# A linear-attention and MLP kernel: batch elements in the row halves of TensorE, attention products on 64x64 quarters, and another draw of the planned order

## The chip, the cores and the metric

The kernel runs on one core of a Trainium2 chip. The core has a matrix engine (TensorE, called PE in the profile), a vector engine (VectorE, DVE), a scalar engine (ScalarE, ACT), a general-purpose engine (GpSimd, POOL) and an engine for synchronisation and DMA issue (SyncE, SP). Each works through its own queue of instructions in order; semaphores tie the queues together. The metric is the time of one execution on the device in microseconds (us).

## The reference

For each of 4 batch elements and 8 heads, a 64x64 state is carried over 768 time steps with a decay per head, and read out with the query:

```python
gamma = 1.0 - 2.0 ** (-5.0 - np.arange(H))
for t in range(S):
    state = gamma * state + einsum('bhd,bhe->bhde', k[:, :, t], v[:, :, t])
    y[:, :, t] = scale * einsum('bhd,bhde->bhe', q[:, :, t], state)
x = y.transpose(0, 2, 1, 3).reshape(B * S, H * D)      # 3072 x 512
h = x @ w_in                                           # 3072 x 2048
out = (h * cos(h)) @ w_out                             # 3072 x 512
```

Inputs and the output are float32; the kernel multiplies in bf16.

## The kernel before

**Tiling.** The recurrence is taken in chunks of 128 time steps, 6 per batch element. A *pair* is one chunk of two batch elements, so there are 12 pairs (`NP`). The decay is folded into q and v (`conv_q`, `conv_v`, by the tables `gq` and `gk`), so that inside a chunk the output is the masked product (Q K^T) V, and what comes from earlier chunks is Q times the state. For each pair the kernel

- loads q, k and v, and converts them to bf16 (`conv_q` L282 and `conv_v` L286 mostly on POOL, `conv_k` on ACT);
- transposes q and k to put the head dimension on the partitions (`qkt`): pairs 0 to 5 on PE (`t_mm`, L308) with a copy out of PSUM (`t_copy`), later pairs by DMA transposes in SP's queue (`dma_t`, L297);
- forms A = K Q^T for the eight heads of both elements (`a_mm`, L331), with two heads in the two row halves of PE, each 64 rows by 128 columns;
- masks A into bf16 (`a_mask`, L337, DVE);
- forms Y = state Q + V A (`y_mm`, L362 and L367) in column halves, 128 rows by 64 columns; the state stands in 128x128 blocks with zeros off the diagonal, `stb`;
- adds to the state in PSUM (`s_mm`, L387, 128x64) and copies it out (`s_copy`);
- copies Y out to `xt` (`y_copy`, ACT).

Two pairs make a *group* of 512 tokens, which runs through the MLP: `f_mm` (L401; `h_mm`, L422, for half a group early on), the cosine on ACT (`f_cos`, L409), the product on DVE (`f_mul`, L413), and the output projection `o_mm` (L446), whose result goes out through `o_out`.

**What sets the order.** Pairs 0 to 5, the transposes and A of pair 6 and the first MLP group are put in order by a planner written in the kernel (`Plan`): each operation has an engine, a cost, a rank and its inputs, the planner simulates the engines, and the operations are emitted by planned start. While PE waits early on, the planner inserts matmuls on zeros (`idle_mm`, L472). The rest is a loop written out by hand: 16 steps per group, each with four matmuls of F for one group and four of O for the group before it, and in every eighth step `block(p)`: A of pair p+1, then Y of pair p, its copies, S, the state copy and the masks. `conv(p + 2)` and the loads of pair p+4 follow. The waits among engines come from the data that instructions share.

**Buffers.** PSUM has seven banks in rotation (`Banks`) and one for the state. q, k, v and `qkt` in bf16 have three sets each, the loads five, the outputs four (`ob`). In the planned part all loads are issued from POOL's queue, between its conversions.

Of the kernel before, what the change touches and what calls it, by code (L numbers as in the profile page):

```python
# [28 lines left out]
class Plan:  # L29
# [33 lines left out]
    def run(self, start, cold_until=0.0, look=0.0, fill=None):  # L63
# [5 lines left out]
        t = 0.0  # L69
        while left:  # L70
            nxt = []
            for e in "SPADE":
# [4 lines left out]
                soon = 1e9  # L77
                for op in left:
# [5 lines left out]
                    if r > t + 1e-9:  # L84
                        nxt.append(r)
                        if op["rank"] < 20:
                            soon = min(soon, r)
                        continue
# [14 lines left out]
                if e == "E" and best and best[0][0] >= 1000 and soon < t + look:  # L103
                    best = None
                if best is None:
# [35 lines left out]

    def emit(self):
        for op in sorted(self.ops, key=lambda o: (o["start"], o["n"])):
            op["fn"](op["eng"])


HALF0, SPARE, RF, RM, COLD = 4, 1, 40.0, 40.0, 5.2
# [3 lines left out]
def kernel(  # L151
# [39 lines left out]
    st_ps = psum.tile([128, 2, HP, D], FP32, name="st_ps")  # L191
# [13 lines left out]
    qs = [sb([128, 2, H, D], BF16, f"qs{i}") for i in range(NB)]  # L205
    ks = [sb([128, 2, H, D], BF16, f"ks{i}") for i in range(NB)]
    vs = [sb([128, 2, H, D], BF16, f"vs{i}") for i in range(NB)]
    qkt = [sb([128, 2, 2, HP, 128], BF16, f"qkt{i}") for i in range(NB)]
    am = [[[sb([128, HP, 128], BF16, f"am{i}_{b}_{j}") for j in range(2)]
           for b in range(2)] for i in range(2)]  # L210
    stb = [sb([128, 2, HP, 128], BF16, f"stb{i}") for i in range(2)]
# [3 lines left out]
    kx = sb([128, 2, H, D], BF16, "kx")  # L215
# [10 lines left out]
    dec = gtf[:, 2048:4096].bitcast(FP32).rearrange("p (j a t) -> p j a t", j=2, a=HP)  # L226
# [4 lines left out]

    def kb(p):
        return kx if p == 1 else ks[p % NB]
# [6 lines left out]
    def load(eng, p, names):  # L240

        bp, c = divmod(ORDER[p], NC)
        for n in names.split():
            t, src = SRC[n[0].lower()]
            if len(n) == 1:
                t = (qs[p % NB] if n == "Q" else kb(p)) if n in "QK" else t[p % PRE]
# [31 lines left out]
    def conv_q(p, b, e):  # L278
        if p < 2:
            copy(e, qs[p % NB][:, b], qf[p % PRE][:, b])  # L280
            return
        ENG[e].tensor_tensor(out=qs[p % NB][:, b], in0=qf[p % PRE][:, b],  # L282
                             in1=bc(gq, ORDER[p] % NC), op=ALU.mult)
# [8 lines left out]
    def conv_k(p, b, e):  # L292
        copy(e, ks[p % NB][:, b], kf[p % PRE][:, b])

    def dma_t(p, w):
        n = p % NB
        nc.sync.dma_start_transpose(  # L297
            out=qkt[n][:, w].rearrange("p b a t -> p (b a) t"),
            in_=(qs, ks)[w][n].rearrange("p b h d -> p (b h d)"))
# [3 lines left out]
    def t_mm(p, b, w):  # L303
        if w == 0:
            held["t", p, b] = banks.take()
        tr = held["t", p, b].bitcast(BF16).rearrange("p (w a t) -> p w a t", w=2, a=HP)
        for a in range(HP):
            nc.tensor.transpose(  # L308
                tr[:, w, a, :], (kb(p) if w else qs[p % NB])[:, b, 2 * a : 2 * a + 2, :], ident)

    def t_copy(p, b, w, e):
        bank = held["t", p, b]
        tr = bank.bitcast(BF16).rearrange("p (w a t) -> p w a t", w=2, a=HP)
        copy(e, qkt[p % NB][:, w, b], tr[:, w])
        if w == 1:
            banks.give(bank)

    def qt(n, b, a):
        return qkt[n][:, 0, b, a, :]

    def kt(n, b, a):
        return qkt[n][:, 1, b, a, :]

    def a_mm(p, b):
        n = p % NB
        bk = held["a", p, b] = [banks.take(), banks.take()]
        ap = [t.rearrange("p (a t) -> p a t", a=HP) for t in bk]
        for a in range(HP):
            for j in range(2):
                po = 64 * j  # L330
                nc.tensor.matmul(ap[j][:, a, :], lhsT=kt(n, b, a)[po : po + 64, :],  # L331
                                 rhs=qt(n, b, a)[po : po + 64, :],
                                 tile_position=(po, 0))

    def a_mask(p, b, j):
        bank = held["a", p, b][j]
        nc.vector.tensor_tensor(  # L337
            out=am[p % 2][b][j], in0=bank.rearrange("p (a t) -> p a t", a=HP),
            in1=(dec[:, j] if p < 2 else mask.unsqueeze(1).to_broadcast([128, HP, 128])),
# [3 lines left out]
    def a_save(p, b, j):  # L343
        bank = held["a", p, b][j]
        nc.scalar.copy(out=amf[b], in_=bank)
        banks.give(bank)

    def a_late(p, b, j):
        nc.gpsimd.tensor_tensor(out=am[p % 2][b][j],
                                in0=amf[b].rearrange("p (a t) -> p a t", a=HP),  # L350
                                in1=dec[:, j], op=ALU.mult)

    def y_mm(p, b):
        c = ORDER[p] % NC
        n = p % NB
        bank = held["y", p, b] = banks.take()
        v_ = vr[p] if p < 2 else vs[n]
        yp = bank.rearrange("p (a t) -> p a t", a=HP)
        for a in range(HP):
            if c > 0:  # L360
                for j in range(2):
                    nc.tensor.matmul(  # L362
                        yp[ts(j, 64), a, :], lhsT=stb[p % 2][:, b, a, ts(j, 64)],
                        rhs=qt(n, b, a), start=True, stop=False,
                        skip_group_check=True)
            for j in range(2):
                nc.tensor.matmul(  # L367
                    yp[ts(j, 64), a, :], lhsT=v_[:, b, 2 * a + j, :],
                    rhs=am[p % 2][b][j][:, a, :], start=(c == 0), stop=True,
                    skip_group_check=True)  # L370
# [10 lines left out]
    def s_mm(p):  # L381
        x = 1 if p == LATE else p
        for b in range(2):
            for a in range(HP):
                for j in range(2):
                    h = 2 * a + j
                    nc.tensor.matmul(  # L387
                        st_ps[ts(j, 64), b, a, :], lhsT=kb(x)[:, b, h, :],
                        rhs=vb(x)[:, b, h, :],
                        start=(ORDER[x] % NC == 0 and b == 0 and a == 0),  # L390
                        stop=True, skip_group_check=True)

    def s_copy(p, j, e):
        copy(e, stb[(max(p, 1) + 1) % 2][ts(j, 64), :, :, ts(j, 64)], st_ps[ts(j, 64)])
# [54 lines left out]
    def o_out(g, j, e):  # L449
# [5 lines left out]
        nc.sync.dma_start(out=out[ds(o_row(g, j), C), :], in_=o)  # L455
# [46 lines left out]
    for j in range(2):  # L502
        for a in range(HP):
            nc.scalar.activation(out=dec[:, j, a, :], in_=dist, func=AF.Exp, bias=lnsc,
                                 scale=float(lg[2 * a + j]))
# [9 lines left out]
    CQ, CD = "D", "P"  # L515
    SPLIT = {(1, 0, 1), (0, 1, 1)}
    HOLD = "q2", "o2"
# [40 lines left out]
    for i in range(2):  # L558
        T["z", i] = add("D", 0.53, lambda e, i=i: nc.vector.memset(stb[i], 0.0), (), 1500, name="z%d" % i)
    for p in range(PL + 2):  # L560
# [26 lines left out]
        if p < DMA_T:  # L587
            for b in range(2):
                for w, x in enumerate("qk"):
                    T["t" + x, p, b] = add(  # L590
                        "E", 0.225, lambda e, p=p, b=b, w=w: t_mm(p, b, w),
                        [T["c" + x, p, b]] + ([T["tq", p, b]] if w else []), 10 * p + 1,
                        [("bank", 1)] if w == 0 else [], (), "full", name="t%s%d%d" % (x, p, b))
                for w, x in enumerate("qk"):
                    T["e" + x, p, b] = add(
                        "DA", SB2, lambda e, p=p, b=b, w=w: t_copy(p, b, w, e),
                        [T["t" + x, p, b], T.get(("eq", p, b)) if w else None] + old,
                        10 * p + 0.5, (), [("bank", 1)] if w else [], name="e%s%d%d" % (x, p, b))
            kq = {b: [T["eq", p, b], T["ek", p, b]] for b in range(2)}
        else:  # L600
# [4 lines left out]
            kq = {b: [T["dt", p, 0], T["dt", p, 1]] for b in range(2)}  # L605
        if p > PL:
            continue
        ms = []
        if p < ASEP:
            for b in range(2):  # L610
                T["a", p, b] = add("E", 0.225, lambda e, p=p, b=b: a_mm(p, b), kq[b], 10 * p + 2,
                                   [("bank", 2)], (), "row", name="a%d%d" % (p, b))
        else:
            T["a", p, 0] = T["a", p, 1] = add(
                "E", 0.445, lambda e, p=p: (a_mm(p, 0), a_mm(p, 1)), kq[0] + kq[1], 10 * p + 2,
                [("bank", 4)], (), "row", name="a%d" % p)
        for b in range(2):
            for j in range(2):
                if (p, b, j) in SPLIT:
                    o = add("A", (0.49, 0.585), lambda e, p=p, b=b, j=j: a_save(p, b, j),  # L620
                            [T["a", p, b]], 0, (), [("bank", 1)],
                            name="ms%d%d%d" % (p, b, j))
                    T["m", p, b, j] = add("P", (1.1, 1.2), lambda e, p=p, b=b, j=j: a_late(p, b, j),
                                          [o], 0, [("port", 1)], [("port", 1)],
                                          name="ml%d%d%d" % (p, b, j))
                    continue
                T["m", p, b, j] = add("D", (0.6, 0.69), lambda e, p=p, b=b, j=j: a_mask(p, b, j),
                                      [T["a", p, b], G("y", p - 2, b)], 10 * p + 1 + b,
# [158 lines left out]
```

## Time and profile before

| | |
|---|---|
| median of 3 runs | 212.67 us (212.4 to 212.92) |
| the profiled execution's own time | 212.12 us |
| its span, first to last instruction | 210.3 us |
| PE busy | 205.1 us (98%), 1726 matmuls |
| DVE, ACT, POOL busy | 116.2, 115.7, 80.0 us |
| O, L446 | 368 matmuls, 128x512 |
| F, L401 / L422 | 304 of 128x512 / 160 of 128x256 |
| A, L331 | 192 matmuls of 64x128 tiles |
| Y, L362 + L367 | 160 + 192 matmuls of 128x64 tiles |
| S, L387 | 160 matmuls of 128x64 tiles |
| matmuls on zeros, L472 | 62 |

In the page's rows of digits each digit is the busy share, in tenths, of one of 40 slices of the span (5.26 us each). In a timeline the first number is the start in us from the span's start, the second the time to the last end; then engine, line, operation, tiles written and read, the shape and the count. Matmuls are pipelined, and their ends are modelled, so the lengths of neighbours overlap and the distance from start to start is what one costs. For SP the rows are DMA issues by its queue ("SPq").

### The profile page before, as it was taken

The numbers are of one execution on the slowest core, as the hardware profiler recorded it, in microseconds if no ns is written. First come the engines' busy times: TensorE is split into PE (matmuls) and PEld (weight loads), VectorE is DVE, ScalarE is ACT, GpSimd is POOL, SyncE is SP. The second block draws the span as 40 slices with busy tenths as digits, with TensorE's granted clock in tenths as the row PEclk, the third lists the DMA queues.
The fourth block names the chain that finished last, engine by engine and source line by source line (L and its number), as shares of the span: only waits on it lengthen the run. The fifth ranks groups of instructions, "written<-read, shape, count | busy, mean of one in ns | idle before, by whom it ended". The sixth has DMA issues, their size and how long they took to land.

```text
span 210.3 us, 4279 instructions
## 1 busy us (share of the span) xinstructions
PE 205.1 (98%) x1726; PEld 112.9 (54%) x1726; DVE 116.2 (55%) x199; ACT 115.7 (55%) x193; POOL 80.0 (38%) x84
## 2 busy tenths in 40 slices
PE   7999999999999999999999999999999999999993
PEld 3777457888565445445445445445444444444462
DVE  7465899988664547647647647647642333333000
ACT  7767869878472347547546546545545554553120
POOL 8969999979999034635033000000000000000000
PEclk9999999999999999999999999999999999999998
DMA  7999999999999399999973303301101101110212
GB/s 118 195 255 230 304 321 218 212 338 345 345 254 204 105 229 255 258 220 246 216 200 103 92 8 104 95 4 55 48 2 53 50 0 50 50 55 10 90 72 78
DMA packets 57492, 32.00 MB, mean 152 GB/s; under 512 B 46592, under 2 KB 51968, under 8 KB 57472
## 3 DMA queue, kind: packets, MB, share of 16 engines
q0 software_dynamic: 14352, 15.47, 33.4%
q1 hardware_dynamic: 42976, 16.13, 30.5%
q8 instruction: 13, 0.21, 0.4%
q10 hardware_dynamic: 144, 0.13, 0.2%
q14 instruction: 7, 0.06, 0.1%
HBM read 27.26 MB, written 6.29 MB: 160 GB/s over the span
## 4 chain that ended last, share of the span: by engine, by line
PE 80%; DMA 7%; POOL 7%; ACT 2%; issue 1%; DVE 1%; POOLq 0%; DVEq 0%; ACTq 0%
PE bank L446 38%; PE bank L401 27%; DMA vf<-in_v_dram 7%; PE bank L422 5%; PE bank L362 2%; PE bank L331 2%; PE bank L367 2%; PE bank L463 2%; PE bank L308 1%; POOL qf L247 1%; POOL kf L247 1%; POOL vs L286 1%; ACT cosb L409 1%; PE st_ps L387 1%; POOL w_in_sb L258 1%
## 5 line engine op out<-in xcount | busy, mean ns | idle before, releaser
L409 ACT ACTIVATE cosb<-bank,halfpi 128x512 bf16<-128x512 f32 x96 | 65.5, 688 | 58.6 <-PE bank L401 54.0
L446 PE MATMUL bank<-w_out_sb,gt 128*128 128x512 bf16 x368 | 90.9, 379 | 0.0
L413 DVE TENSOR_TENSOR gt<-bank,cosb 128x512 bf16<-128x512 f32 x76 | 51.6, 689 | 54.0 <-ACT cosb L409 53.7
L401 PE MATMUL bank<-xt,w_in_sb 128*128 128x512 bf16 x304 | 77.1, 379 | 0.0
L446 PEld LDWEIGHTS <-gt 128*128 128x128 bf16 x368 | 35.6, 98 | 42.3
L401 PEld LDWEIGHTS <-w_in_sb 128*128 128x128 bf16 x304 | 28.8, 98 | 33.6
L286 POOL TENSOR_TENSOR vs<-vf,gk 128x512 bf16<-128x512 f32 x22 | 22.7, 1048 | 11.1 <-PE st_ps L387 4.8
L337 DVE TENSOR_TENSOR am<-bank,mask 128x512 bf16<-128x512 f32 x40 | 25.0, 683 | 1.8 <-PE bank L331 1.6
L282 POOL TENSOR_TENSOR qs<-qf,gq 128x512 bf16<-128x512 f32 x18 | 18.5, 1044 | 18.7 <-DMA qf<-in_q_dram 18.6
L271 ACT COPY ob<-bank 128x512 f32<-128x512 f32 (+1 forms) x24 | 13.8, 577 | 17.4 <-PE bank L446 16.2
L273 DVE CAST stb<-st_ps 64x512 bf16<-64x512 f32 x19 | 13.0, 686 | 11.8 <-PE st_ps L387 11.5
L422 PE MATMUL bank<-xt,w_in_sb 128*128 128x256 bf16 x160 | 19.0, 273 | 0.2 <-ACT xt L271 0.2
L422 PEld LDWEIGHTS <-w_in_sb 128*128 128x128 bf16 x160 | 15.2, 98 | 2.4 <-issue 0.3
L271 ACT CAST xt<-bank 128x512 bf16<-128x512 f32 x24 | 12.9, 589 | 6.2 <-PE bank L367 6.2
L430 DVE TENSOR_TENSOR gt<-bank,cosb 128x512 bf16<-128x512 f32 x20 | 13.5, 688 | 4.6 <-ACT cosb L409 4.4
L271 ACT CAST ks<-kf 128x512 bf16<-128x512 f32 x20 | 11.6, 622 | 3.1 <-DMA kf<-in_k_dram 3.1
L472 PE MATMUL bank<-zero 128*128 128x256 bf16 (+1 forms) x62 | 11.0, 316 | 1.2 <-DVE halfpi L488 1.1
L362 PE MATMUL bank<-qkt,stb 128*64 128x128 bf16 x160 | 10.3, 222 | 0.0
L367 PE MATMUL bank<-am,vs 128*64 128x128 bf16 x160 | 10.0, 219 | 0.0
L362 PEld LDWEIGHTS <-stb 128*64 128x64 bf16 x160 | 8.7, 110 | 2.4 <-issue 1.9
L247 POOL DMA_DIRECT2D vf<-in_v_dram x8 | 9.4, 1185 | 0.0
L367 PEld LDWEIGHTS <-vs 128*64 128x64 bf16 x160 | 8.9, 110 | 0.0
(59 smaller groups left out, 113.0 us busy)
## 6 DMA issues: line engine op xcount, KB each, us to landing
out_dram<-ob SPq DMA_DIRECT2D x23, 256.0 KB, 2.1
vf<-in_v_dram POOLq DMA_DIRECT2D x8, 512.0 KB, 8.6
qf<-in_q_dram POOLq DMA_DIRECT2D x6, 512.0 KB, 9.7
kf<-in_k_dram POOLq DMA_DIRECT2D x6, 512.0 KB, 9.7
w_out_sb<-in_moe_w_out_dram POOLq DMA_DIRECT2D x4, 512.0 KB, 11.3
qf<-in_q_dram SPq DMA_DIRECT2D x4, 512.0 KB, 4.6
kf<-in_k_dram SPq DMA_DIRECT2D x4, 512.0 KB, 6.1
vf<-in_v_dram SPq DMA_DIRECT2D x4, 512.0 KB, 6.3
```

The lines of the kernel that those rows point to most:

```text
L247: eng.dma_start(out=t.rearrange("p b h d -> p (b h) d"), in_=src[ds(2 * bp, 2), :, ds(c * C, C), :].rearrange("b h t d -> t (b h) d"))
L271: nc.scalar.copy(out=out, in_=in_)
L282: ENG[e].tensor_tensor(out=qs[p % NB][:, b], in0=qf[p % PRE][:, b], in1=bc(gq, ORDER[p] % NC), op=ALU.mult)
L286: ENG[e].tensor_tensor(out=vb(p)[:, b], in0=vf[p % PRE][:, b], in1=bc(gk, ORDER[p] % NC), op=ALU.mult)
L337: nc.vector.tensor_tensor(out=am[p % 2][b][j], in0=bank.rearrange("p (a t) -> p a t", a=HP), in1=(dec[:, j] if p < 2 else mask.unsqueeze(1 ...
L362: nc.tensor.matmul(yp[ts(j, 64), a, :], lhsT=stb[p % 2][:, b, a, ts(j, 64)], rhs=qt(n, b, a), start=True, stop=False, skip_group_check=True)
L367: nc.tensor.matmul(yp[ts(j, 64), a, :], lhsT=v_[:, b, 2 * a + j, :], rhs=am[p % 2][b][j][:, a, :], start=(c == 0), stop=True, skip_group_c ...
L401: nc.tensor.matmul(bank, lhsT=w_in_sb[:, i, ts(f, 128)], rhs=xt[g % 2][:, i, :], start=(i == 0), stop=(i == KIN - 1))
L409: nc.scalar.activation(out=cb, in_=bank, func=AF.Sin, bias=halfpi)
L413: nc.vector.tensor_tensor(out=gt[g % 2][:, f, :], in0=bank, in1=cb, op=ALU.mult)
L422: nc.tensor.matmul(bank[:, ts(e, 256)], lhsT=w_in_sb[:, i, ts(f + e, 128)], rhs=xt[g % 2][:, i, ts(hf, 256)], start=(i == 0 and e == 0), s ...
L446: nc.tensor.matmul(bank, lhsT=gt[g % 2][:, f, ts(j, 128)], rhs=w_out_sb[:, f, :], start=(f == 0), stop=(f == KOUT - 1))
```

## The change

The layout of q and k in bf16 turns from (element, head) to (head, element), so that from pair 2 on one transpose gives both batch elements of one head, element 0 on partitions 0 to 63 and element 1 on 64 to 127. Heads were side by side there before. A and Y now use 64x64 quarters of PE: row half by batch element (or by half of the time steps), column half by output half. The state needs no zeros (`stb` is 8 heads of 64 columns), and it is copied out by one instruction on all partitions instead of two on half of them.

Y has three sorts of products. The state part takes element b in row half b. The part inside the chunk splits its 128 source steps into two row halves; the later half reaches only the later 64 output columns. Both halves add to the same bank, so an element's second half must come after its first: `y1_mm` does one half of each element, `y2_mm` the other, and an empty instruction in another engine's queue (`hop`), which waits for the last matmuls of `y1_mm` and is waited for by `y2_mm`, stands between them. It is in SP's queue for pairs up to 5 and in POOL's after that. In `block`, and in the plan for pairs 4 and 5, A of the next pair stands between `y1_mm` and `y2_mm`; for pairs 2 and 3 it is S, and for pair 11 nothing.

In the plan, the transposes of one pair half are one operation (q and k, both elements) for pairs 2 to 5; the v conversions of pair 2 go from POOL to DVE; two holds on loads change; all ranks get a random addition from a fixed seed, and POOL and DVE may wait for an operation of better rank that is nearly ready. The issue of an output DMA is split from the copy and follows block, conversions and loads of its step in the hand-written loop.

```diff
+    def jitter(self, seed, by):
+        r = random.Random(seed)
+        for op in self.ops:
+            op["rank"] += by * r.random()
...
+SEED, JIT, HOLD = 41, 4.0, "PD"
...
-    qs = [sb([128, 2, H, D], BF16, f"qs{i}") for i in range(NB)]
-    ks = [sb([128, 2, H, D], BF16, f"ks{i}") for i in range(NB)]
+    qs = [sb([128, H, 2, D], BF16, f"qs{i}") for i in range(NB)]
+    ks = [sb([128, H, 2, D], BF16, f"ks{i}") for i in range(NB)]
...
-    stb = [sb([128, 2, HP, 128], BF16, f"stb{i}") for i in range(2)]
+    stb = [sb([128, H, D], BF16, f"stb{i}") for i in range(2)]
...
-    def a_mm(p, b):
+    def a_mm(p, u):
         n = p % NB
-        bk = held["a", p, b] = [banks.take(), banks.take()]
+        bk = held["a", p, u] = [banks.take(), banks.take()]
         ap = [t.rearrange("p (a t) -> p a t", a=HP) for t in bk]
         for a in range(HP):
-            for j in range(2):
-                po = 64 * j
-                nc.tensor.matmul(ap[j][:, a, :], lhsT=kt(n, b, a)[po : po + 64, :],
-                                 rhs=qt(n, b, a)[po : po + 64, :],
-                                 tile_position=(po, 0))
+            h = 4 * u + a
+            for x in range(1 if p < 2 else 2):
+                for b in range(2):
...
+                    nc.tensor.matmul(ap[b][ts(x, 64), a, :], lhsT=kt(n, b, h)[:, ts(x, 64)],
+                                     rhs=qt(n, b, h), tile_position=(64 * b, 64 * x),
+                                     skip_group_check=True)
...
+    def intra(p, b, a, x, **kw):
+        ms = []
+        for j in range(2):
+            h = 2 * a + j
+            ms.append(nc.tensor.matmul(
+                held["yp", p][b][ts(j, 64), a, 64 * x :], lhsT=vs[p % NB][ts(x, 64), b, h, :],
+                rhs=am[p % 2][b][h // 4][ts(x, 64), h % 4, 64 * x :],
+                start=False, stop=True, tile_position=(64 * x, 64 * j), skip_group_check=True))
+        return ms
+
+    def y1_mm(p):
...
+        for a in range(HP):
+            for b in range(2):
+                for j in range(2):
+                    h = 2 * a + j
+                    nc.tensor.matmul(
+                        held["yp", p][b][ts(j, 64), a, :], lhsT=stb[p % 2][ts(b, 64), h, :],
+                        rhs=qt(p % NB, b, h), start=(a == 0), stop=False,
+                        tile_position=(64 * b, 64 * j), skip_group_check=True)
+        for a in range(HP):
+            held["part", p] = intra(p, 1, a, 1) + intra(p, 0, a, 0)
+
+    def hop(p):
+        ms = held["part", p]
+        held["hop", p] = (nc.sync if p <= 5 else nc.gpsimd).nop(nofuse=True)
+        for m in ms:
+            after(m, held["hop", p])
+
+    def y2_mm(p):
+        for a in range(HP):
+            for m in intra(p, 1, a, 0) + intra(p, 0, a, 1):
+                if a == 0:
+                    after(held["hop", p], m)
...
-    CQ, CD = "D", "P"
-    SPLIT = {(1, 0, 1), (0, 1, 1)}
-    HOLD = "q2", "o2"
+    MERGE = 4
+    CQ, CD = "D", "D"
+    SPLIT = {(1, 1, 0), (0, 1, 1)}
+    HM, HCQ, HCV = "q2", "", ""
...
+            def y(e, p=p, a_next=a_next):
+                y1_mm(p)
+                hop(p)
+                if a_next:
+                    a_mm(p + 1, 0)
+                    a_mm(p + 1, 1)
+                    y2_mm(p)
+                if has_s(p):
+                    s_mm(p)
+                if not a_next:
+                    y2_mm(p)
...
     def block(p):
         nxt = p + 1 < NP
+        y1_mm(p)
+        hop(p)
         if nxt:
             a_mm(p + 1, 0)
             a_mm(p + 1, 1)
+        y2_mm(p)
         for b in range(2):
-            y_mm(p, b)
             y_copy(p, b, "A")
         if has_s(p):
             s_mm(p)
-            for j in range(2):
-                s_copy(p, j, "D")
+            s_copy(p, "D")
...
                 if p + 4 < NP:
                     load(nc.sync, p + 4, "q k v")
+            if s % 4 == 3:
+                o_dma(g - 1, s // 4)
```

`after` adds a dependency by hand between two instructions. The order of operations in the built program, as far as the text below speaks of it: 62 matmuls on zeros as before; then, between the transposes of pair 3 and block 6, `H x8, half of A3, O x4, half of A3, O x4, H x16, Y3 with S, H x64, 16 transposes of pair 4, O x4, H x8, A4, O x8, H x32, O x8, 16 transposes of pair 5, O x12, Y4 with A5 and S, O x16, Y5 with A6 and S, O x8`, and four times `F x4, O x4`.

## The prediction

> **What bounds the kernel now.** I read the page's busy rows and slices first, then the chain that ended last, then PE's waits, then timelines of one stage each.
>
> ```profile
> PE   7999999999999999999999999999999999999993
> ...
> POOL 8969999979999034635033000000000000000000
> ...
> DMA  7999999999999399999973303301101101110212
> ...
> PE 80%; DMA 7%; POOL 7%; ACT 2%; issue 1%; DVE 1%; POOLq 0%; DVEq 0%; ACTq 0%
> ```
>
> PE is full almost everywhere, POOL and DMA until about 68 us. Before 34 us the chain runs through DMA landings and POOL; after 34.3 us it is PE alone. All waits of PE together are 1.5 us, but line 472, 62 matmuls on zeros (11.0 us, nearly all before 15.7 us), is filler: useful PE work starts at 15.70 us. So from there on a us of PE work is a us of the span, as long as PE is fed. One step of the steady stage:
>
> ```profile
> 93.30 1.03 PE L446 MATMUL bank<-w_out_sb,gt 128*128 128x512 bf16 x4
> 94.26 0.62 PE L331 MATMUL bank<-qkt 64*128 64x128 bf16 x16
> 94.81 0.25 PE L362 MATMUL bank<-qkt,stb 128*64 128x128 bf16 x2
> ...
> 95.73 0.42 PE L387 MATMUL st_ps<-vs,ks 128*64 128x64 bf16 x16
> 96.08 1.04 PE L401 MATMUL bank<-xt,w_in_sb 128*128 128x512 bf16 x4
> ```
>
> Columns are start and length; lengths overlap, so starts count. Four 512-column matmuls take 0.864, so the output projection ends at 94.16 and A begins 0.10 later: a change of tile shape costs about 0.09. A takes 0.55 with the next change in it: 0.45 for 16, 28 ns each. Y, 32 matmuls, takes 0.92 (28.7 ns), S 0.25 for 16 (15.6 ns) and then 0.10 of change. A 128-column matmul on the whole array takes 56 ns (8 transposes from 58.43 to 58.88). So two half tiles already run side by side, in rows (A) and in columns (Y). The block costs 96.08 - 94.16 = 1.92.
>
> **What the Trainium skill says.** "TensorEngine Tiling (Array Packing)", Key Properties: changing the tile shape drains the array; the trace agrees (0.09). "TensorE: Matmul & The Clock Gate", Measured speedup vs the span model: row and column tiles compose, at about 4 ns per extra tile; the trace shows each direction alone, not both. The same page, "Wait — 56ns, not 53.3ns?", puts a floor of about 25 ns between starts; S at 15.6 ns contradicts it for half tiles, and the measurement decides, but quarters are not shown. "PSUM — Partial Sum Buffer", PSUM bank collisions: row tiles may not write one bank at once, software must order them. That is why the change needs its hand-over; no run shows a collision.
>
> **The change, part by part.** (Pair p: two batch elements and one chunk.)
>
> *Blocks.* New order: Y1, hand-over, A of the next pair, Y2, S. Y1 is 16 state matmuls on four quarters, 4 rounds of 56 ns = 0.22, and the first intra half, 4 rounds = 0.22 (64 columns on the other row half hide beside 128). A is 32 quarters in 8 rounds = 0.45; Y2 0.22; S 0.25; three shape changes 0.28. Sum 1.65 against 1.92, 0.27 less. One wait may eat 0.03: A's last bank is the one that L401 filled last, whose DVE multiply ends at 94.91, and A's second half would start at 94.16 + 0.09 + 0.44 + 0.22 = 94.91. I take 0.24 for each of pairs 6 to 10: -1.2. Pair 11 has no A: 1.09 (0.09 + 0.90 + 0.10) becomes 0.67 + 0.19 + an uncovered hand-over of 0.29 = 1.15: +0.05.
>
> *Hand-over.* Last result 0.16 after its slot (a 56 ns matmul shows as 0.22), about 0.03 until another engine sees it (L401 ends at 93.47, its cosine starts at 93.50), 0.06 in that queue, 0.04 back (last two estimates from gaps between sequencer entries): 0.29. It is covered by A (0.45) from pair 4 on, and by S with its two changes (0.43) for pairs 2 and 3: nothing. Without cover, 0.29 each. On POOL (pairs 6 on) the q and v conversions of pair p+2 now queue behind it, so they start in block p instead of earlier; they take 4.1 and the DMA transposes about 4, within a step of 15.7: nothing.
>
> *Planned part, pairs 2 to 5.* Before: A as four pieces of (0.22 + 0.19) and three of (0.45 + 0.19) = 3.56; four Y with S at 1.34 = 5.36; sum 8.92. After: A2 in one piece 0.64, A3 in two 0.82, A4 0.64; pairs 2 and 3 need four changes, 0.45 + 0.25 + 0.22 + 0.37 = 1.29 each; pairs 4 and 5 hold the next A, 1.65 each; sum 7.98. That is -0.94.
>
> So PE loses about 2.1 us of work: 208.2 if it is never starved. DVE's state copy becomes one instead of two (0.69 less per pair, two memsets fewer), off the path. Two v conversions move from POOL to DVE (1.2), before 35 us. Output DMAs move behind block, transposes and loads in SP's queue; four output buffers hide it.
>
> *Feeding.* All 16 transposes of pair 4 now stand in one piece, and each takes both batch elements' q. Before, the first four took element 0 alone and H work stood between:
>
> ```profile
> 42.21 6.29 PE L422 MATMUL bank<-xt,w_in_sb 128*128 128x256 bf16 x56
> 48.36 0.40 PE L308 MATMUL bank<-ident,qs 128*128 128x128 bf16 x4
> 48.59 1.04 PE L422 MATMUL bank<-xt,w_in_sb 128*128 128x256 bf16 x8
> ```
>
> POOL's q conversions of that pair are the two L282 rows:
>
> ```profile
> 43.39 1.15 POOL L247 DMA_DIRECT2D qf<-in_q_dram  x1
> 46.08 1.15 POOL L247 DMA_DIRECT2D kf<-in_k_dram  x1 [1.54 <-issue]
> 47.25 1.06 POOL L282 TENSOR_TENSOR qs<-qf,gq 128x512 bf16<-128x512 f32 x1
> 48.23 1.19 POOL L247 DMA_DIRECT2D vf<-in_v_dram  x1
> 49.44 1.06 POOL L282 TENSOR_TENSOR qs<-qf,gq 128x512 bf16<-128x512 f32 x1
> ```
>
> The new program has the same order there. Removing two conversions (2.0) ahead does not help: the load at 46.08 waits 1.54 though nothing in the profile holds it, and starts 0.33 after the landing at 45.75 in the trace's landing records; landings then come every 1.52, DMA being full. So the second half is ready at 50.50 again. PE gets there when? From 15.70: H x32 and one filler 3.8, F x48 10.4, transposes x32 1.8, S 0.44, A 1.46, blocks 2 and 3 2.58, H x88 9.6, O x8 1.7: 47.5. I expect 1 to 2 us of waits before it (DVE is 92 to 96% busy from 20 to 40 us and gets more), which cost nothing up to 3.0. So PE stands until 50.55. From there to block 6: transposes 0.89, O x4 0.86, H x8 0.87, A4 0.64, O x8 1.73, H x32 3.50, O x8 1.73, transposes 0.89, O x12 2.59, block 4 1.65, O x16 3.46, block 5 1.65, ten groups of O or F 8.64: 29.10, and 0.09: Y of pair 6 starts at 79.74. Its counterpart before started at 78.52. **PE is 1.2 late at block 6**, the 0.94 and more already spent.
>
> *SP's queue.* For pairs 4 and 5 the hand-over stands behind DMA transposes that wait for POOL:
>
> ```profile
> 62.10 1.24 SPq L297 DMA_TRANSPOSE qkt<-qs  x1
> 63.39 0.58 SPq L455 DMA_DIRECT2D out_dram<-ob  x1
> ...
> 66.10 2.27 SPq L297 DMA_TRANSPOSE qkt<-qs  x1
> ```
>
> Pair 4's is free at 64.0; Y1 ends at 50.55 + 13.70 + 0.54 = 64.8: no wait. Pair 5's follows two transposes from 66.1 (1.24 to 2.27 each, the rows above) and an output: 69.1 to 71.2; Y2 wants it at 70.35. I take 0.1.
>
> Sum: 1.2 - 1.2 + 0.05 + 0.1, near +0.2: span 210.5, profiled execution 212.12 + 0.2 = 212.3. The median of the runs is 212.67, 0.55 above that execution; the forecast for the median is 212.9.
>
> **Rivals.** (1) *PE isn't starved at 50.5.* For it: the 1.54 idle is unexplained, and POOL is 2 us ahead. Against: the landing times. If the load goes out at 44.54, the conversion ends 1.5 earlier; but pair 4's hand-over holds Y2 until 64.1 instead of 65.2, so 1.1 at most comes back: 211.8. (2) *Quarters don't run four at a time*, slower: 14 ns each is assumed, S showed 15.6. After 50.5 us there are 640 quarter matmuls: 15.6 gives +1.0 (213.9), 17.4 eats the whole gain of a block (+2.2, 215.0), 25 would give +7. From 14.5 on it decides against the kernel. (3) *The hand-over is longer than its cover*: nothing until 0.45, then 0.7 us of span per 0.1 on seven blocks; 0.6 gives 213.9. (4) *More starving*: over 3 us of waits before 50.5, or SP's transposes at 2.27 each: 213.5 to 214.5.
>
> **How the numbers follow.** Forecast 0.40 (of it 0.32 within 0.2%, 0.06 slower, 0.02 faster), (1) 0.20 (0.18 faster), (2) 0.18, (3) 0.12, (4) 0.10. Measurement can't tell 0.2%, 0.43 us. Faster 0.20, same 0.36, slower 0.44. Range: below 211.4 lie the best of (1) and unforeseen gains, 0.1; above 215.0 the worst of (2) and (3), 0.1. The forecast's own range is 212.4 to 213.5.
>
> **What would show it.** Right: a PE wait near 49 to 50.5 us before the transposes, released by POOL; block 6 about 1.2 later than 78.5; steps of 15.49 instead of 15.73; Y2 never waiting except in pair 11. Wrong: A's 32 quarters well over 0.45, a gap ahead of Y2 in each block, or pair 4's transposes starting before 50.

## The result and the profile after

The changed kernel takes 212.44 us (median of 4 runs, 212.11 to 212.68) and the kernel before, measured beside it, 212.59 us. The ratio is 0.999, 95% interval 0.9971 to 1.0009: no difference that this measurement can tell. A second comparison with more runs (14 and 33) gives 1.0009, 0.9996 to 1.0023. The forecast was 212.9 us with a range of 212.4 to 213.5, and "within 0.2%" as the likely answer of this main case; over all its cases together the prediction gave "slower" 0.44 and "same" 0.36.

The profiled execution took 212.52 us with a span of 210.7 us, 0.4 more than that of before. From the page of the changed kernel, in the parts shown of before (span, busy time, slices, chain):

```profile
span 210.7 us, 4885 instructions
...
PE 203.6 (97%) x2046; PEld 111.8 (53%) x2046; DVE 109.7 (52%) x189; ACT 115.4 (55%) x193; POOL 78.0 (37%) x82
...
PE   7998989998999999999999999999999999999993
...
POOL 8889969979998007007007007000000000000000
...
PE 78%; POOL 10%; DMA 4%; issue 3%; DVE 2%; ACT 1%; POOLq 0%; DVEq 0%
```

PE's busy time fell by 1.5 us, yet the span did not shorten. The slice from 47.4 to 52.7 us (the tenth digit) is now an 8, like the fourth and the sixth, and POOL's share of the chain grew from 7% to 10%. PE's waits (total in us, how many, the longest) say what stands there:

```profile
PE bank L546 <- DVE halfpi L562: 1.1, 1, 1.1
PE bank L337 <- POOL qs L308: 0.7, 1, 0.7
PE bank L472 <- DVE am L372: 0.6, 1, 0.6
PE bank L493 <- DMA w_in_sb<-in_moe_w_in_dram: 0.6, 1, 0.6
PE bank L493 <- ACT xt L297: 0.3, 1, 0.3
```

The first line stands in both kernels, at the start. The second is the wait that the prediction named; the other three come earlier, at 30, 17 and 36 us. In the timeline of PE around it (first start, length, then in brackets the idle time ahead):

```profile
42.39 7.16 PE L493 MATMUL bank<-xt,w_in_sb 128*128 128x256 bf16 x64
50.23 0.40 PE L337 MATMUL bank<-ident,qs 128*128 128x128 bf16 x4 [0.68 <-POOL qs L308]
...
79.58 0.42 PE L428 MATMUL bank<-qkt,stb 64*64 64x128 bf16 x16
```

Block 6 of the kernel before:

```profile
78.52 0.62 PE L331 MATMUL bank<-qkt 64*128 64x128 bf16 x16
```

POOL's timeline of the changed kernel for the same time:

```profile
45.75 1.15 POOL L273 DMA_DIRECT2D kf<-in_k_dram  x1 [1.56 <-issue]
46.92 1.06 POOL L308 TENSOR_TENSOR qs<-qf,gq 128x512 bf16<-128x512 f32 x1
47.90 1.19 POOL L273 DMA_DIRECT2D vf<-in_v_dram  x1
49.12 1.05 POOL L308 TENSOR_TENSOR qs<-qf,gq 128x512 bf16<-128x512 f32 x1
```

The two conversions of q4 stand behind a load issue each. The first load also waits 1.56 us, for nothing that the profile names; it starts 0.34 after q4's landing at 45.41 in the landing records, as the load before did 0.33 after its landing at 45.75. Why stays open. The second conversion ends at 50.17, and the transposes start at 50.23. Block 6 then starts at 79.58, 1.06 later than before.

One step of the steady stage of the changed kernel:

```profile
94.19 1.03 PE L517 MATMUL bank<-w_out_sb,gt 128*128 128x512 bf16 x4
95.14 0.42 PE L428 MATMUL bank<-qkt,stb 64*64 64x128 bf16 x16
...
95.58 0.69 PE L366 MATMUL bank<-qkt 64*64 64x128 bf16 x30
96.06 0.43 PE L414 MATMUL bank<-am,vs 64*64 64x128 bf16 x16
96.42 0.44 PE L460 MATMUL st_ps<-vs,ks 128*64 128x64 bf16 x16
96.79 0.39 PE L472 MATMUL bank<-xt,w_in_sb 128*128 128x512 bf16 x1
```

The output projection's slots end at 94.19 + 0.864 = 95.05, and F starts at 96.79: the block takes 1.74 us, 0.18 less than before. From the start of S in one step to that in the next it is 15.57 us; before it was 15.74. So the account of the span is: +1.06 up to block 6, five steps of -0.171 = -0.86, pair 11 +0.08, together +0.28. The last output projection (L537, L463 before) starts at 203.40 us against 203.12, which is that sum; 0.1 more comes in the last 7 us.

### The profile page after: what moved, and what is told of

Same layout as the page of the kernel before. It is cut to its first block, busy times and chain, and to the rows that moved or that the text cites. A ratio compares the mean times of both kernels' runs of the same rounds, so it can differ in the third digit from the quotient of the medians.

```text
span 210.7 us, 4885 instructions
## 1 busy us (share of the span) xinstructions
PE 203.6 (97%) x2046; PEld 111.8 (53%) x2046; DVE 109.7 (52%) x189; ACT 115.4 (55%) x193; POOL 78.0 (37%) x82
## 4 chain that ended last, share of the span: by engine, by line
PE 78%; POOL 10%; DMA 4%; issue 3%; DVE 2%; ACT 1%; POOLq 0%; DVEq 0%
PE bank L517 37%; PE bank L472 29%; DMA w_in_sb<-in_moe_w_in_dram 4%; PE bank L493 3%; POOL vf L273 3%; PE bank L366 2%; PE bank L414 2%; POOL qs L308 2%; PE bank L537 2%; PE st_ps L460 1%; PE bank L428 1%; POOL qf L273 1%; POOL vs L312 1%; POOL vx L312 1%; PE bank L337 1%
## 5 line engine op out<-in xcount | busy, mean ns | idle before, releaser
L472 PEld LDWEIGHTS <-w_in_sb 128*128 128x128 bf16 x304 | 29.1, 98 | 34.4 <-issue 0.6
L297 ACT COPY ob<-bank 128x512 f32<-128x512 f32 (+1 forms) x24 | 13.9, 578 | 15.7 <-PE bank L517 14.5
L312 POOL TENSOR_TENSOR vs<-vf,gk 128x512 bf16<-128x512 f32 x20 | 20.7, 1047 | 0.3
L493 PEld LDWEIGHTS <-w_in_sb 128*128 128x128 bf16 x160 | 15.4, 98 | 3.8 <-DMA w_in_sb<-in_moe_w_in_dram 0.8
L299 DVE CAST stb<-st_ps 128x512 bf16<-128x512 f32 x10 | 6.9, 688 | 11.1 <-PE st_ps L460 11.1
L414 PE MATMUL bank<-am,vs 64*64 64x64 bf16 (+1 forms) x320 | 8.2, 205 | 0.1
L546 PEld LDWEIGHTS <-zero 128*128 128x128 bf16 x62 | 6.1, 106 | 4.0 <-issue 2.0
L297 ACT COPY qkt<-bank 128x512 bf16<-128x512 bf16 x12 | 6.6, 587 | 2.1 <-PE bank L337 2.1
L273 POOL DMA_DIRECT2D kf<-in_k_dram x6 | 7.1, 1182 | 1.6 <-issue 1.6
```

The lines of the kernel that those rows point to most:

```text
L273: eng.dma_start(out=t.rearrange("p b h d -> p (b h) d"), in_=src[ds(2 * bp, 2), :, ds(c * C, C), :].rearrange("b h t d -> t (b h) d"))
L297: nc.scalar.copy(out=out, in_=in_)
L312: ENG[e].tensor_tensor(out=vb(p)[:, b], in0=vf[p % PRE][:, b], in1=bc(gk, ORDER[p] % NC), op=ALU.mult)
L472: nc.tensor.matmul(bank, lhsT=w_in_sb[:, i, ts(f, 128)], rhs=xt[g % 2][:, i, :], start=(i == 0), stop=(i == KIN - 1))
L493: nc.tensor.matmul(bank[:, ts(e, 256)], lhsT=w_in_sb[:, i, ts(f + e, 128)], rhs=xt[g % 2][:, i, ts(hf, 256)], start=(i == 0 and e == 0), s ...
L546: nc.tensor.matmul(bank[:, : 256 * n].rearrange("p (n t) -> p n t", n=n), lhsT=zero[:, :128], rhs=zero.unsqueeze(1).to_broadcast([128, n, ...
```

## The experiments

The changed kernel ran again beside the first group of experiments as their control:

> The changed kernel as it is, on the same chip and in the same rounds as the three that follow, so that each is set against it. Expected: 212.4 us, as on record, and the first transpose of pair 4 at about 50.2 us after a wait of 0.6 to 0.7 us for POOL.

It took 212.52 us (14 runs), with the first transpose of pair 4 at 50.27 after a wait of 0.63. The experiments from "A back on row halves" on ran in other rounds, beside the kernel before (212.56 us, and 212.32 for the last one) but not beside the changed kernel, so their differences from it are differences of medians of separate rounds. Steps below are taken from start of S to start of S, in one profiled execution each.

**POOL's order at 45 to 50 us, both ways.** In the plan's result the two loads k6 and v6 are put behind the second conversion of q4 (`cq41`):

```diff
+    by = {o["name"]: o for o in plan.ops}
+    by["k6"]["start"] = by["cq41"]["start"] + 1e-6
+    by["v6"]["start"] = by["cq41"]["start"] + 2e-6
     plan.emit()
```

> POOL converts both halves of q4 before it issues the loads k6 and v6; nothing else moves. Theory: the 0.68 us that TensorE waits at pair 4's transposes is due only to POOL's order, and behind it the span is a fixed sum of TensorE work. Then the transposes start where TensorE arrives, at about 49.55 us, and the span falls by up to 0.68 us; by 0.4 to 0.5 us if the hand-over of pair 4 on SP or the two later loads give part of it back. Time about 211.9 us. Rival: another wait (the loads k6 and v6 landing later, SP's queue) takes the place of this one, and the time stays at 212.4 us within 0.2.

And the opposite, one more load (q7) ahead of that conversion:

```diff
+    by = {o["name"]: o for o in plan.ops}
+    by["cq41"]["start"] = by["q7"]["start"] + 1e-6
+    for x in ("t40", "t41"):
+        by[x]["start"] = max(by[x]["start"], by["cq41"]["start"] + 2e-6)
     plan.emit()
```

> The opposite: POOL issues one more load ahead of its second conversion of q4, about 1.2 us of POOL's time. Theory (what is late at pair 4's transposes goes whole to the end): the wait there grows from 0.68 to about 1.9 us and the time by 1.0 to 1.2 us, to about 213.5 us. Rival (the wait is slack that a later stage would have spent anyway): under 0.3 us.

Measured: 211.74 us, ratio to before 0.9965 (0.9956 to 0.9974), 0.78 less than the control; and 213.59 us, 1.0055 (1.0039 to 1.0071), 1.07 more. POOL and then PE with the loads behind:

```profile
45.64 2.03 POOL L308 TENSOR_TENSOR qs<-qf,gq 128x512 bf16<-128x512 f32 x2 [1.37 <-DMA qf<-in_q_dram]
47.62 1.19 POOL L273 DMA_DIRECT2D kf<-in_k_dram  x1
48.81 1.15 POOL L273 DMA_DIRECT2D vf<-in_v_dram  x1
```

```profile
42.74 7.16 PE L493 MATMUL bank<-xt,w_in_sb 128*128 128x256 bf16 x64
49.74 0.39 PE L337 MATMUL bank<-ident,qs 128*128 128x128 bf16 x4
...
79.08 0.42 PE L428 MATMUL bank<-qkt,stb 64*64 64x128 bf16 x16
```

PE with one more load ahead:

```profile
51.37 0.40 PE L337 MATMUL bank<-ident,qs 128*128 128x128 bf16 x4 [1.70 <-POOL qs L308]
```

With the loads behind, the conversions start as soon as q4 lands, at 45.64; the first load in the profile above started at 45.75, so the wait of 1.56 ahead of it was not what made q4 late, but the two issues (1.15 and 1.19) were.

The transposes find their data without a wait, and block 6 starts 0.50 earlier than above. The saving is larger than the 0.68 in brackets would allow, because a bracket counts from the modelled end of the last matmul: here the 64 matmuls ahead take 7.00 from start to start, so in the profile above the transposes could have started at 42.39 + 7.00 = 49.39, and they started 0.84 later. In the execution with the loads behind, PE came there 0.35 later, for it had lost 0.4 us more to a load of weights near 17 us (1.0 instead of 0.6); 0.84 - 0.35 is the 0.50 of this profile, and 0.84 is near the 0.78 of the medians. No wait shows up later for it: neither the later loads nor SP's queue takes anything back. With one more load the wait grows by 1.07 (from the control's 0.63) and the time by 1.07. So, within the intervals, this one place in POOL's queue goes one to one to the end, and the rival (slack that is spent anyway) falls in both directions.

**The hand-over without cover.** In the blocks of pairs 6 to 10, A goes ahead of Y1:

```diff
-        y1_mm(p)
-        hop(p)
         if nxt:
             a_mm(p + 1, 0)
             a_mm(p + 1, 1)
+        y1_mm(p)
+        hop(p)
         y2_mm(p)
```

> In the blocks of pairs 6 to 10, A of the next pair is put ahead of the state part of Y, so that state part, hand-over and intra part of Y stand directly behind one another and nothing covers the hand-over. Theory of the prediction (a hand-over without cover costs about 0.3 us, estimated, and A covers it wholly in the changed kernel): five blocks by 0.3 us, the time rises by about 1.4 us, and a gap of about 0.3 us ahead of the intra part shows in each block. Rival (the hand-over is passed while PE drains its own pipeline and needs no cover): under 0.3 us in all.

Measured: 214.83 us, 1.0116 (1.0099 to 1.0132), 2.3 us over the control; the step is 16.04, 0.47 longer. The timeline of weight loads (PEld) and matmuls in one block of this kernel, and DVE's multiply of the last F:

```profile
95.74 0.64 PE L366 MATMUL bank<-qkt 64*64 64x128 bf16 x32
96.21 0.65 PE L428 MATMUL bank<-qkt,stb 64*64 64x128 bf16 x16
96.45 0.25 PEld L428 LDWEIGHTS <-stb 64*64 64x64 bf16 x13 [0.18 <-issue]
96.65 0.91 PE L414 MATMUL bank<-am,vs 64*64 64x128 bf16 x32
97.14 0.25 PEld L414 LDWEIGHTS <-vs 64*64 64x64 bf16 x16 [0.27 <-POOLq L437]
97.49 0.44 PE L460 MATMUL st_ps<-vs,ks 128*64 128x64 bf16 x16
```

```profile
95.70 0.69 DVE L484 TENSOR_TENSOR gt<-bank,cosb 128x512 bf16<-128x512 f32 x1 [1.03 <-ACT cosb L480]
```

Two things show, and the expectation had only one. The hand-over holds the second half of Y for 0.27 (estimated: 0.29). And Y1 itself stops for 0.18 after its first matmuls. The profile names no releaser for that ("issue"). The banks rotate, so in this order Y1 gets the bank that the last F filled; its DVE multiply ends at 96.39, and Y1 goes on 0.06 after that. This reading rests on these times alone. 0.27 + 0.18 = 0.45 of the 0.47. So the order of the block gives two covers: one for the hand-over, and one for a bank that comes free late.

**A back on row halves.** A alone on 64x128 tiles, by taking the branch of pairs 0 and 1 for all:

```diff
-            for x in range(1 if p < 2 else 2):
+            for x in range(1):
                 for b in range(2):
-                    if p < 2:
+                    if True:
```

> A alone is put back on 64x128 row halves (16 matmuls instead of 32 quarters); Y stays on quarters, and the order of the block stays. Theory: A's own time is 0.45 us either way (16 by 28 ns, or 8 rounds of 56 ns), so quarters bring nothing but the absence of two changes of tile shape inside the block, 0.09 to 0.10 us each: 0.19 us for each of the blocks of pairs 4 to 10, together 1.3 us, time about 213.8 us. Rival 1 (quarters run slower than row halves in the block, and the gain of the change is from its order alone): no change or faster. Rival 2 (quarters are themselves faster): over 2 us.

Measured: 213.70 us, 1.0064 (1.0041 to 1.0087), 1.2 over the changed kernel. One block of it on PE:

```profile
95.57 0.42 PE L428 MATMUL bank<-qkt,stb 64*64 64x128 bf16 x16
95.82 0.39 PE L414 MATMUL bank<-am,vs 64*64 64x128 bf16 x16
96.14 0.62 PE L363 MATMUL bank<-qkt 64*128 64x128 bf16 x16
96.69 0.41 PE L414 MATMUL bank<-am,vs 64*64 64x128 bf16 x16
97.03 0.44 PE L460 MATMUL st_ps<-vs,ks 128*64 128x64 bf16 x16
```

The step is 15.75, 0.185 longer: in size, the two changes of tile shape at 0.09 that were expected. They may cost a little more: the changed kernel waits 0.04 per step for a bank inside A (next experiment), and on row halves A's second half seems to come too late for that wait; then the two changes are 0.22. That is also the step of the kernel before (15.74). All that quarters save for A is that its neighbours have the same shape; with A on row halves, the saving in Y is eaten by the two changes that Y1 and Y2 around A then bring.

**F directly ahead of the block.** In the steps with a block the last F goes behind the output projection:

```diff
-            if g < NG:
...
+            late = p < NP and r == 3
+            if g < NG and not late:
                 f_mm(g, s)
...
             if s % 4 == 3:
                 o_out(g - 1, s // 4, "A")
+            if late:
+                f_mm(g, s)
+                f_cos(("f", g, s))
+                f_mul(g, s)
```

> In the five steps with a block, the output projection and its copy are put ahead of the last input projection F, so that F stands directly ahead of the block and the bank that A's second half needs was filled earlier. Theory: the pause of 0.16 us in one row half of A, which starts again 0.03 us after DVE's multiply has ended, is a wait for that bank, and it costs 0.05 to 0.1 us of each step; without it the time falls by 0.2 to 0.5 us. Rival: the other row half fills the time and the pause costs nothing, or the first bank of the block is now the late one: no change, or up to 0.5 us slower.

The pause in question does not show on a grouped line of PE; in single records one row half of A starts nothing between 95.70 and 95.86, while the other goes on. What was suspected is this multiply in DVE's timeline of the changed kernel, which frees A's last bank at 95.80:

```profile
95.11 0.69 DVE L484 TENSOR_TENSOR gt<-bank,cosb 128x512 bf16<-128x512 f32 x1 [1.04 <-ACT cosb L480]
```

DVE and PE with F last:

```profile
93.43 0.69 DVE L484 TENSOR_TENSOR gt<-bank,cosb 128x512 bf16<-128x512 f32 x1 [1.03 <-ACT cosb L480]
96.02 0.69 DVE L484 TENSOR_TENSOR gt<-bank,cosb 128x512 bf16<-128x512 f32 x1 [1.90 <-ACT cosb L480]
```

```profile
95.19 0.42 PE L428 MATMUL bank<-qkt,stb 64*64 64x128 bf16 x16
...
96.42 0.44 PE L460 MATMUL st_ps<-vs,ks 128*64 128x64 bf16 x16
```

Now the multiply before the block ends at 94.12, long ahead of A. Both row halves run through, and Y1 to S takes 1.23 instead of 1.28; the step is 15.53. So the pause was that bank, at 0.04 per step, just under the low end of the expectation. The time, 212.34 us, 0.9994 (0.9984 to 1.0004), is the same by itself: 5 x 0.04 = 0.2 us is what this measurement can hardly tell.

**Both gains together.** The edits "loads behind the conversions" and "F directly ahead of the block" in one kernel:

> Both edits that were expected to gain: POOL converts both halves of q4 ahead of the loads k6 and v6, and the output projection stands ahead of the last F in the steps with a block. Theory: the stages are apart and each saving goes whole to the end, so the savings add: 0.74 us measured for the first, 0.2 to 0.5 us expected of the second, time about 211.4 us. Rival: the first alone, 211.7 us.

Measured: 211.48 us, 0.9962 (0.9946 to 0.9978), the lowest median here, and faster than the kernel before by its interval, than the changed kernel by the larger of that kernel's two comparisons. Against the first edit alone (0.9965) the second adds nothing that the intervals can tell; only the shorter steps speak for it.

**The hand-over on SP's queue.**

```diff
-        held["hop", p] = (nc.sync if p <= 5 else nc.gpsimd).nop(nofuse=True)
+        held["hop", p] = nc.sync.nop(nofuse=True)
```

> The hand-over of pairs 6 to 11 is put back on SP's queue, where those of pairs 2 to 5 are. Theory: in a step of the changed kernel SP's queue has two output DMAs ahead of it, the second of which waits for ACT's copy of the output projection and ends at 97.4 us, while Y2 wants to start at 96.1 us. So Y2 waits about 1.0 to 1.4 us in each of the blocks of pairs 6 to 10, and the time rises by 4 to 8 us; the place of the hand-over in a queue is then worth more than all that the blocks save. Rival: SP's queue catches up when PE is late, and Y2 waits for less than 0.3 us a block: under 1.5 us.

Measured: 219.42 us, 1.0322 (1.0297 to 1.0348). The size is as expected and the place is not, so that the size fits is luck. PE, then SP's queue, in the block of pair 6:

```profile
80.47 0.69 PE L366 MATMUL bank<-qkt 64*64 64x128 bf16 x30
85.52 0.64 PE L414 MATMUL bank<-am,vs 64*64 64x128 bf16 x16 [4.36 <-SPq L437]
86.08 0.64 PE L460 MATMUL st_ps<-vx,kx 128*64 128x64 bf16 x16
```

```profile
78.50 2.19 SPq L273 DMA_DIRECT2D qf<-in_q_dram  x1
80.79 2.82 SPq L273 DMA_DIRECT2D kf<-in_k_dram  x1
83.70 1.71 SPq L273 DMA_DIRECT2D vf<-in_v_dram  x1
```

A single wait of 4.36 us, in the first block alone, behind the six loads of pairs 8 and 9, which the expectation had not counted in SP's queue; the rows are the last three, those of pair 9, and the wait ends when the last has been issued. (The prediction had read the DMA engines as full until about 68 us; the row that it shows has nines again from 74 to 105 us, where these loads and the next ones fall.) In the next blocks PE is late enough for the queue, and Y2 no longer waits; the outputs never held it. Part of the rest is PE's clock, in a table of stretches (time, then busy time and count of PE, PEld, DVE, ACT and POOL, then the granted clock, the DMA share and GB/s):

```profile
84.00:85.50 1.50, 0.00 (x0) 0.00 (x0) 0.00 (x0) 0.00 (x0) 1.04 (x2) 0.89 0.84 192
85.50:86.50 1.00, 0.98 (x32) 0.82 (x32) 0.00 (x0) 0.29 (x1) 0.89 (x1) 0.50 1.21 275
...
87.50:88.50 1.00, 1.00 (x3) 0.44 (x3) 1.00 (x2) 0.82 (x2) 0.15 (x1) 0.50 1.22 277
88.50:89.50 1.00, 1.00 (x6) 0.39 (x4) 1.00 (x3) 0.69 (x1) 0.00 (x0) 0.95 0.50 113
```

By this table the clock fell to 0.50 at about 85.2 us, 4.0 us after the last matmul's end, and came back at about 88.6. Y2 took 0.56 instead of 0.36, and the step from this S to the next 16.70, 1.14 more than a steady one. Y2 would have started at 80.47 + 0.48 = 80.95 and was 4.57 late; with the 0.2 and the 1.14, and block 6 having begun 0.4 later than in the control, that is the 6.3 us by which this span exceeds the control's. The Trainium skill, "TensorE: Matmul & The Clock Gate", What's actually happening, says that PE runs at half its clock after at least one idle window of about 3.4 us; this trace agrees, and so does the kernel with one more load ahead, which idled 1.70 us and kept a clock of 1.00.

**The plan without the random addition.**

```diff
-SEED, JIT, HOLD = 41, 4.0, "PD"
+SEED, JIT, HOLD = 41, 0.0, "PD"
```

> The random addition to the ranks is set to nothing (4.0 to 0.0), so that the planned part (pairs 0 to 5) is laid out by plain ranks; the hand-written steps behind it are as in the changed kernel. Theory: the matmuls are the same in number and size, POOL still has the loads k6 and v6 between the two conversions of q4, and the pick of the order moves only waits ahead of pair 4's transposes, which POOL's wait there swallows up to 0.7 us: time within about 1 us of 212.5, steps of 15.56 as before. Rival: the pick is what makes this layout work, and without it TensorE starves somewhere before 72 us: over 214.5 us, with a new wait of more than 1 us in the list of waits.

Measured: 212.45 us, 1.0000 (0.9986 to 1.0014), steps of 15.56: the same, as the theory had it. Its list of waits has the same cause at its head, longer in the execution that was profiled, which was the slowest of its runs (213.19):

```profile
PE bank L337 <- POOL qs L308: 1.3, 1, 1.3
```

So this seed's order is worth nothing that can be measured against the order by plain ranks. The other changes in the plan (the holds, the v conversions on DVE) were not tested one by one.

## Why the prediction was right

**Blocks: right in kind, mis-sized.** The prediction had 1.65 for a block and took 0.24 off; it is 1.74, 0.18 off. Its parts against the timeline above: Y1 0.44 (as predicted), A 0.48 instead of 0.45, Y2 with its change of shape 0.36 instead of 0.31, S with its change 0.37 instead of 0.34. The term "one wait may eat 0.03" was that of A's last bank: it is real, and 0.04 per step by the experiment that took it away. The other 0.05 over 1.65 lies at Y2, S and their changes of shape, and its cause was not found. Five blocks give -0.9, not -1.2. Rival (2), quarters that don't run four at a time, is refuted: with that bank's wait gone, Y1, A and Y2 take 1.23 with one change of shape, 1.14 for 80 matmuls or 14.3 ns each, below the 14.5 from which it would have decided (with the wait, 1.28 gives 14.9). In single records quarters start in fours, 3 to 4 ns apart, once in 56 ns; S starts in pairs, after the first once in 28 to 32 ns. So S's mean of 15.6 ns did not contradict, as the prediction held, a floor of 25 ns, if that is meant for one tile.

**Hand-over: right.** Y2 waits in no block of the changed kernel but pair 11's (+0.08, predicted +0.05), and uncovered it costs 0.27 (predicted 0.29), in pair 11 as in the experiment. Rival (3) needed over 0.45. What the prediction did not see is that the same order also covers a bank.

**Feeding: right in place and mechanism, off by 0.3 us in when, and by 0.1 in what it cost.** It had PE standing until 50.55, at the transposes of pair 4, for POOL's second conversion; it was 50.23, and block 6 was 1.06 late instead of 1.2. Of that lateness, POOL's order accounts for 0.84 us in starts, 0.78 by the experiment's medians. Even without it block 6 would come no earlier than before, so the 0.94 that the prediction counted as saved in the planned part is gone too: ahead of the transposes PE waited 0.55 for weights, 0.62 for DVE's masks and 0.30 for ACT's copy of `xt`, against 0.22 in the kernel before. What in the plan makes these three waits was not tested. The prediction also held that two conversions fewer ahead on POOL would bring nothing, because the load before q4's conversion waits in any case: it waited 1.54 before and 1.56 after. Rival (1) is the experiment with the loads behind the conversions: its bound of 1.1 us held, with 0.78 measured. The 1 to 2 us of waits allowed ahead of the transposes were about 2: PE arrived at 49.4 to 49.55, the bare sum was 47.5. Rival (4), over 3 us of them, did not come.

**SP's queue: over-counted.** The 0.1 taken for pair 5's hand-over is not there; both planned blocks run through. But the caution was apt: the same queue from pair 6 on cost 6.9 us, for loads that the prediction did not name.

**The sum.** Predicted span +0.2, measured +0.4 in the profiled execution; the medians differ by -0.15 and, in the larger comparison, by nothing. That the sum came out so close is in part luck: the blocks saved 0.3 less than predicted, and the feeding and SP's queue cost 0.14 and 0.1 less. The forecast of 212.9 lay 0.5 above the result: 0.1 to 0.3 of it because it started from a median of three runs of before, 212.67, which more runs put at 212.3 to 212.6.

## What to carry to other kernels

Where one engine is full, an order of work that saves on it only pays if it is still fed: here the 0.9 us saved in the steps was all lost again ahead of them, most of it at one place, where two loads are issued around one conversion; moving these two brought 0.78 us. Packing into smaller tiles is worth what the change of shape beside it leaves: ask which neighbours share the shape. A hand-over through another queue cost 0.27 us here, and nothing with 0.45 us of other matmuls behind it; but then it must be a queue with nothing slow ahead, DMA issues above all. A wait that the profile puts in brackets can cost more than its figure, here 0.84 for 0.68.

## What the runs showed of the hardware that was not expected

A load's issue in SP's queue took 1.7 to 2.8 us in a stretch where the DMA engines were full (the rows of pair 9; the DMA share from 80 to 85 us is 1.03), and an empty instruction behind six loads waited for all of them. One long idle stretch of TensorE cost more than its length: 4.36 us were followed by a loss of 1.3 us at half the clock (0.2 in Y2, 1.14 in the step).
